# Attention and gated MLP on one core: pairs 4, 5 and 6 of batch 1 brought back to x^T by the transposing DMA in place of five transposes and a copy each

## The chip, the cores and the metric

The kernel runs on one core of a Trainium2 chip. The metric is device time in microseconds (us). Before the change: 323.52 us, the median of three runs (323.32 to 324.7). The program is one launch; its five engines (TensorE for matmuls, VectorE, ScalarE, GpSimd, and SyncE, which here only issues DMAs) each work through their own list of instructions and wait for one another by semaphores.

## The reference

Two layers follow each other. The first is causal attention with a sliding window of 128 and a linear bias, for 8 batches of 8 heads, 576 positions and 64 channels:

```
scores = q @ k^T / 8 - slope[h] * |i - j|      kept where 0 <= i - j < 128
attn   = exp(scores - max) / sum
x      = attn @ v        -> one row of 512 per token, 4608 tokens
```

The second is a gated MLP with 2048 hidden units:

```
h   = x @ w_in                   512 -> 2048
out = (h * clip(h + 3, 0, 6) / 6) @ w_out      2048 -> 512
```

## The kernel before

**Units.** Heads are taken two at a time. A *pair* g is batch g // 4 and heads 2(g % 4) and 2(g % 4) + 1; there are 32. Pairs 4 to 7 are batch 1, and `NP` is 4. For each pair the kernel makes the scores (TensorE), their exponentials (ScalarE), masks them (GpSimd), multiplies them with v (TensorE) and divides by the row sum (VectorE, L413 in `attend` for batches 0 and 1, L402 in `values` for the others). The divided tile is called `avs`: 128 tokens on the partitions, five blocks of tokens, two heads of 64 channels.

**Back to x^T.** The MLP wants x with channels on the partitions. `back(g)` (L421) turns `avs` into the rows of `xT` that belong to the pair, in one of two ways:
- by TensorE: five transposes of 128 x 128 into a PSUM tile (L432) and a copy from there into `xT` (L438; ScalarE, or VectorE for pair 7);
- by a transposing DMA from `avs` to `xT`, issued by SyncE (L425). It writes 640 columns, of which the last 64 are later overwritten by the next batch.

`by_xbar(g)` (L418) chooses: the DMA for pairs from 8 on, except 10 and 11; TensorE for all the others.

**Buffers.** `avs` comes from the pool `small`, which has two buffers in turn:

```
    small = ctx.enter_context(tc.tile_pool(name="small", bufs=2))
...
        avs = st[g, "avs"] = small.tile([128, NQ, 2, D], BF16, tag="avs", name="avs")
```

So `avs` of pair g takes the place of pair g - 2. The wide PSUM tiles of scores and values come from `ps_sc`, also two buffers; `wide_double` (L248, transposes of the next batch's q or k) uses the same pool.

**The MLP.** Tokens are taken 512 at a time (nt = 0 to 8). `up_mms` (L444) multiplies four blocks of 128 rows of `w_in` with four blocks of `xT`, one for each pair of a batch; L470 (ScalarE) and L471 (VectorE) make the gate; L501 is the second matrix; L510 and L511 copy and store the result. `up_begin(nt, ms, 3)` does the first three of the four blocks, and so reads the first three pairs of a batch. Tokens 512 to 1023 (nt = 1) need batch 1.

**Order.** The order of the work is written out by hand: inside `manual_schedule` every engine, SyncE among them, executes what the code gives it in the order of the code. The MLP's steps are laid between the attention's by `fill(n)`, which takes the next n steps of a fixed list and stops at a step whose batch isn't counted complete in `done[0]` (L528). `done` steers only this list, at the time the program is built.

**Around the change.** `second_batch` (L618) makes pairs 4 to 7. Ahead of the values it issues, in this order, on SyncE: v of batch 2 (L639, five loads), k of batch 3 (L642, four) and q of batch 3 (L643, five). The first of these waits for a one-column write by GpSimd (L638). Only then come the values and `back`:

```
        attend(NP)
        ...
        attend(NP + 1)
        fill(1)
        back(NP)
        attend(NP + 2)
        fill(1)
        back(NP + 1)
        double(2, 0, "k", 0, "av", A)
        attend(NP + 3)
        back(NP + 2)
        double(2, 0, "k", 1, "av", A)
        wide_double(2, 0, "q", A)
        up_begin(1, 0, 3)
        back(2 * NP - 1)
```

After that `segment` (L669) runs pairs 8 to 31. At its start for each g it sets `done[0] = g - 1` if pair g - 2 goes by the DMA.

Of the kernel before, what the change touches and what calls it, by code (L numbers as in the profile page):

```python
# [18 lines left out]
def kernel(  # L19
# [16 lines left out]
    NP = H // 2  # L36
# [11 lines left out]
    XB = 2 * NP  # L48
# [134 lines left out]
    def cast_tokens(b, nm):  # L183
        s = ld[b, nm]
        if nm == "v":
            for lo in (0, 2):
                nc.gpsimd.tensor_copy(  # L187
                    out=vbuf[b % 2][:, lo:lo + 2, :, 0:D].rearrange("p j h d -> p (j h) d"),
                    in_=s[:, lo:lo + 2, :, :].rearrange("p j h d -> p (j h) d"))
            nc.gpsimd.tensor_copy(out=vbuf[b % 2][:LAST, 4, :, 0:D], in_=s[:LAST, 4, :, :])  # L190
            return
        for j in range(NQ):
            m = min(128, S - j * 128)
            nc.gpsimd.tensor_copy(out=tbuf[:m, :, j, :],  # L194
                                  in_=s[:m, j, :, :].rearrange("p (i e) d -> p i (e d)", e=2))
# [40 lines left out]
    def double(b, dp, nm, part, tag, copy):  # L236
        src = st[b, dp, nm]
        t0, t1 = ((0, 5), (5, RT))[part]
        tp = BANKS[tag].tile([128, t1 - t0, 128], BF16, tag=tag, name="tp2",
                             padded_shape=[128, 8, 128])  # L240
        for t in range(t0, t1):
            nc.tensor.transpose(tp[:, t - t0, :], src[:, t, :], ident)
        dst = (qTb if nm == "q" else kTb)[b % 2][:, 2 * dp:2 * dp + 2, :, :]
        copy(out=dst.rearrange("p i j c -> p i (j c)")[:, :, 0:S].rearrange(  # L244
                 "p i (a t) -> p i a t", t=RT)[:, :, :, t0:t1],
             in_=tp.rearrange("p t (a i) -> p i a t", i=2))
# [83 lines left out]
    def scores(g):  # L330
        scores_diag(g)
        scores_off(g)
# [10 lines left out]
    def exp_diag(g, e):  # L343
        h = 2 * (g % NP) + e
        pd, sc = st[g, "pd"], st[g, "scd"]
        if diag_tabled(g):
            if e == 0:
                nc.scalar.activation(out=pd.rearrange("p e j c -> p e (j c)"), in_=sc,
                                     func=ACT.Exp, scale=scale)
            return  # L350
        nc.scalar.activation(out=pd[:, e, :, :].rearrange("p j c -> p (j c)"),  # L351
                             in_=sc[:, e, :], func=ACT.Exp,
                             bias=bias_d[:, h:h + 1], scale=scale)
        nc.gpsimd.affine_select(out=pd[:, e, :, :], in_=pd[:, e, :, :],  # L354
                                pattern=[[0, 4], [1, 128]], channel_multiplier=-1, base=0,
                                compare_op=ALU.is_ge, fill=0.0)

    def exp_off(g, e):
        h = 2 * (g % NP) + e
        po, sc, p4 = st[g, "po"], st[g, "sco"], p4buf[g % 2]  # L360
        nc.scalar.activation(out=po[:, e, :, :].rearrange("p j c -> p (j c)"),  # L361
                             in_=sc[:, e, :], func=ACT.Exp,
                             bias=bias_o[:, h:h + 1], scale=scale)
        nc.gpsimd.affine_select(out=po[:, e, :, :], in_=po[:, e, :, :],  # L364
                                pattern=[[0, 4], [-1, 128]], channel_multiplier=1, base=-1,
                                compare_op=ALU.is_ge, fill=0.0)
        nc.scalar.activation(out=p4[:, e, 0:64], in_=sc[:, e, 64:128], func=ACT.Exp,  # L367
                             bias=bias_d[:, h:h + 1], scale=scale)
        if e == 1:
            nc.gpsimd.affine_select(out=p4[:, :, 0:64], in_=p4[:, :, 0:64],  # L370
                                    pattern=[[0, 2], [1, 64]], channel_multiplier=-1, base=0,
                                    compare_op=ALU.is_ge, fill=0.0)
# [21 lines left out]
    def values(g, qts):  # L394
        av = ps_av.tile([128, 3, 2, W], FP32, tag="av", name="av", padded_shape=[128, 3, 2, 85])
        nq = len(qts)
        av_matmuls(g, qts, lambda qt, e: av[:, qt - qts[0], e, :])
        if qts[0] == 0:
            st[g, "avs"] = small.tile([128, NQ, 2, D], BF16, tag="avs", name="avs")
        rc = small.tile([128, 3, 2, 1], FP32, tag="rc", name="rc")  # L400
        nc.vector.reciprocal(rc[:, 0:nq, :, :], av[:, 0:nq, :, D:W])
        nc.vector.tensor_tensor(  # L402
            out=st[g, "avs"][:, qts[0]:qts[0] + nq, :, :], in0=av[:, 0:nq, :, 0:D],
            in1=rc[:, 0:nq, :, :].to_broadcast([128, nq, 2, D]), op=ALU.mult)
# [11 lines left out]
    done = [0]  # L416

    def by_xbar(g):  # L418
        return g >= XB and g != XB + 2 and g != XB + 3

    def back(g):  # L421
        b, hp = divmod(g, NP)
        avs = st[g, "avs"].rearrange("p j e d -> p j (e d)")
        if by_xbar(g):
            nc.sync.dma_start_transpose(  # L425
                out=xT[:, hp, ds(b % 4 * S, SP)].rearrange("p (j c) -> p j c", j=NQ),
                in_=avs.rearrange("p j c -> p (j c)"))
            return
        pool, tag = (ps_o, "o") if b < 2 else (ps_h, "h")
        tp = pool.tile([128, SP], BF16, tag=tag, name="tb", padded_shape=[128, 1024])  # L430
        for j in range(NQ):
            nc.tensor.transpose(tp[:, ts(j, 128)], avs[:, j, :], ident)  # L432
        if g == NP - 1:
            nc.scalar.copy(out=xT[:, hp, ds(b % 4 * S, 256)], in_=tp[:, 0:256])
            nc.vector.tensor_copy(out=xT[:, hp, ds(b % 4 * S + 256, S - 256)], in_=tp[:, 256:S])
            return
        eng = nc.vector.tensor_copy if g == 2 * NP - 1 else nc.scalar.copy
        eng(out=xT[:, hp, ds(b % 4 * S, S)], in_=tp[:, 0:S])  # L438
# [84 lines left out]
    def fill(n):  # L523
        for _ in range(n):
            if at[0] == len(units):
                return
            nt, fn, step = units[at[0]]
            if fn is moe_up and done[0] < NP * (min((nt * NT + NT - 1) // S, B - 1) + 1):  # L528
                return
            fn(nt if fn is moe_up else nt - 1, step)  # L530
            at[0] += 1
# [137 lines left out]
    def segment(lo, hi, fills):  # L669
        for g in range(lo, hi + 1):  # L670
            f = fills(g)
            if by_xbar(g - 2):
                done[0] = g - 1
            if lo < g < hi and g != 3 * NP + 1:
                scores(g)
            turn = {2 * NP: (2, 1, "k"), 2 * NP + 1: (2, 1, "q"),
                    2 * NP + 2: (3, 0, "k"), 2 * NP + 3: (3, 1, "k")}.get(g)
            if turn:
                double(*turn, 0, "av", A)
            fill(f[0])  # L680
            if turn:
                double(*turn, 1, *(("h", V) if turn[0] == 2 else ("av", A)))
            if g < hi:
                exp_diag(g, 0)
            fill(f[1])
            if g < hi:
                exp_diag(g, 1)
            if g == 3 * NP:
                cast_tokens(3, "v")
            if g > lo:  # L690
                values(g - 1, (0, 1, 2))
            fill(f[2])
            if g < hi:
                exp_off(g, 0)
            fill(f[3])
            if g < hi:
                exp_off(g, 1)
            if g > lo:
                values(g - 1, (3, 4))
            fill(f[4])  # L700
            if g > lo and by_xbar(g - 1):
                back(g - 1)
            fill(f[5])
            if g < hi:
                stage_next(g)
            fill(1)
            if g == 3 * NP:
                scores(g + 1)
            if g > lo and not by_xbar(g - 1):
                back(g - 1)  # L710
                done[0] = g
            fill(f[6] - 1)
# [51 lines left out]
```

## Time and profile before

| | |
|---|---|
| median of three runs | 323.52 us (323.32 to 324.7) |
| the profiled execution | 323.3 us, its span 321.6 us |
| granted TensorE clock over it | 0.998 |
| busy: TensorE / ScalarE / VectorE / GpSimd | 312.4 / 195.6 / 173.0 / 141.1 us |
| transposing DMAs to `xT` | 22, all on SyncE |
| transposes of `avs` on TensorE (L432) | 50, of 219 ns each as recorded |
| copies to `xT` after them (L438) | 8 on ScalarE, 639 ns; 1 on VectorE, 458 ns |

How to read the profile: times are microseconds from the span's start, unless marked ns. PE is TensorE, PEld its weight loads, DVE VectorE, ACT ScalarE, POOL GpSimd, SPq the instruction queue of SyncE. A row of the timeline gives the start, the length, the engine, the line of the kernel and the operation with its output and inputs, and, in brackets, how long the engine was idle before it and who released it. A row by stage gives the stage, its length, the busy time of TensorE, its weight loads, VectorE, ScalarE and GpSimd (with the number of instructions), the granted TensorE clock, the share of the DMA engines' time and GB/s. Recorded lengths of TensorE's matmuls overlap one another; the distance from one start to the next is what TensorE spends on one.

### The profile page before, as it was taken

The numbers are of one execution on the slowest core, as the hardware profiler recorded it, in microseconds if no ns is written. First come the engines' busy times: TensorE is split into PE (matmuls) and PEld (weight loads), VectorE is DVE, ScalarE is ACT, GpSimd is POOL, SyncE is SP. The second block draws the span as 40 slices with busy tenths as digits, with TensorE's granted clock in tenths as the row PEclk, the third lists the DMA queues.
The fourth block names the chain that finished last, engine by engine and source line by source line (L and its number), as shares of the span: only waits on it lengthen the run. The fifth ranks groups of instructions, "written<-read, shape, count | busy, mean of one in ns | idle before, by whom it ended". The sixth has DMA issues, their size and how long they took to land.

```text
span 321.6 us, 7050 instructions
## 1 busy us (share of the span) xinstructions
PE 312.4 (97%) x2738; PEld 167.6 (52%) x2738; DVE 173.0 (54%) x338; ACT 195.6 (61%) x334; POOL 141.1 (44%) x249
## 2 busy tenths in 40 slices
PE   7889999999999999999999999999999999999996
PEld 5565465455555554554667654554554444444443
DVE  6667674554456555555555555555655455455510
ACT  3758976877767766766676667666764344244401
POOL 8455493594493767366745665463331000000000
PEclk9999999999999999999999999999999999999999
DMA  7999999899999999999999989922112200000112
GB/s 276 202 333 208 247 270 196 210 258 194 212 248 166 244 201 203 193 229 199 192 199 202 237 173 212 214 72 86 23 53 66 75 34 35 33 33 33 67 53 77
DMA packets 131425, 51.90 MB, mean 161 GB/s; under 512 B 118976, under 2 KB 123328, under 8 KB 131392
## 3 DMA queue, kind: packets, MB, share of 16 engines
q1 hardware_dynamic: 126160, 45.36, 66.2%
q0 software_dynamic: 4224, 4.19, 8.2%
q10 hardware_dynamic: 1008, 1.90, 1.6%
q8 instruction: 21, 0.34, 0.5%
q14 instruction: 12, 0.10, 0.1%
HBM read 36.70 MB, written 9.44 MB: 143 GB/s over the span
## 4 chain that ended last, share of the span: by engine, by line
PE 82%; DMA 10%; SPq 2%; POOL 2%; DVE 1%; ACT 1%; issue 1%; POOLq 0%
PE ops L501 37%; PE hps L451 33%; DMA w_out_sb<-in_moe_w_out_dram 5%; DMA ldbuf<-in_v_dram 3%; PE scd L296 3%; DMA ldbuf<-in_k_dram 2%; PE av L391 2%; SPq L112 2%; PE av L383 2%; PE sco L328 1%; PE ops L482 1%; PE w L153 1%; POOL w_out_sb L171 1%; PE tp L219 0%; ACT kTb L244 0%
## 5 line engine op out<-in xcount | busy, mean ns | idle before, releaser
L471 DVE SCALAR_TENSOR_TENSOR gbuf<-r,hps 128x512 bf16<-128x512 f32 x144 | 98.7, 687 | 102.5 <-ACT r L470 100.2
L470 ACT ACTIVATE r<-hps,bias 128x512 f32<-128x512 f32 x144 | 98.9, 689 | 88.9 <-PE hps L451 88.7
L451 PE MATMUL hps<-xT,w_in_sb 128*128 128x512 bf16 (+1 forms) x640 | 144.8, 358 | 0.5 <-ACT xT L438 0.3
L501 PE MATMUL ops<-w_out_sb,gbuf 128*128 128x512 bf16 x560 | 137.8, 379 | 0.3 <-DMA w_out_sb<-in_moe_w_out_dram 0.3
L451 PEld LDWEIGHTS <-w_in_sb 128*128 128x128 bf16 x640 | 59.2, 98 | 54.8 <-issue 0.8
L501 PEld LDWEIGHTS <-gbuf 128*128 128x128 bf16 x560 | 51.8, 98 | 56.7 <-issue 0.6
L354 POOL TENSOR_SCALAR_AFFINE_SELECT pd<-pd 128x512 bf16<-128x512 bf16 x48 | 29.7, 634 | 34.5 <-ACT pd L351 34.5
L364 POOL TENSOR_SCALAR_AFFINE_SELECT po<-po 128x512 bf16<-128x512 bf16 x48 | 30.3, 636 | 32.5 <-ACT po L361 32.3
L351 ACT ACTIVATE pd<-scd,bias_d 128x512 bf16<-128x512 f32 x48 | 31.7, 685 | 4.7 <-PE scd L296 4.7
L510 DVE COPY osb<-ops 128x512 f32<-128x512 f32 x33 | 22.7, 687 | 20.4 <-PE ops L501 20.2
L361 ACT ACTIVATE po<-sco,bias_o 128x512 bf16<-128x512 f32 x48 | 33.0, 688 | 0.0
L194 POOL CAST tbuf<-ldbuf 128x512 bf16<-128x512 f32 (+1 forms) x45 | 25.6, 614 | 16.7 <-DMA qTb<-tbuf 9.0
L402 DVE TENSOR_TENSOR avs<-av,rc 128x384 bf16<-128x384 f32 (+1 forms) x48 | 23.6, 491 | 1.6
L391 PEld LDWEIGHTS <-pd 128*128 128x128 bf16 x192 | 14.3, 97 | 8.3 <-issue 0.5
L383 PE MATMUL av<-vbuf,po 128*128 128x65 bf16 x192 | 18.0, 193 | 0.0
L391 PE MATMUL av<-vbuf,pd 128*128 128x65 bf16 x192 | 17.3, 194 | 0.3 <-ACT kTb L244 0.3
L187 POOL CAST vbuf<-ldbuf 128x1024 bf16<-128x1024 f32 x14 | 14.3, 1044 | 4.3 <-DMA ldbuf<-in_v_dram 4.3
L383 PEld LDWEIGHTS <-po 128*128 128x128 bf16 x192 | 14.3, 98 | 2.9 <-DVE avs L402 0.5
L367 ACT ACTIVATE p4buf<-sco,bias_d 128x64 bf16<-128x64 f32 x48 | 15.5, 324 | 0.0
L227 POOL CAST pr<-ldbuf 128x576 bf16<-128x576 f32 x20 | 12.9, 670 | 5.0 <-DMA ldbuf<-in_k_dram 3.1
L296 PE MATMUL scd<-qTb,kTb 64*128 64x128 bf16 x256 | 12.7, 219 | 1.7 <-DVE kTb L220 0.9
L296 PEld LDWEIGHTS <-kTb 64*128 64x128 bf16 x256 | 7.2, 94 | 13.4 <-issue 9.7
(96 smaller groups left out, 217.4 us busy)
## 6 DMA issues: line engine op xcount, KB each, us to landing
out_dram<-osb SPq DMA_DIRECT2D x33, 256.0 KB, 2.4
ldbuf<-in_v_dram SPq DMA_DIRECT2D x32, 256.0 KB, 5.6
ldbuf<-in_q_dram SPq DMA_DIRECT2D x20, 256.0 KB, 4.9
ldbuf<-in_k_dram SPq DMA_DIRECT2D x16, 256.0 KB, 4.5
ldbuf<-in_q_dram SPq DMA_DIRECT2D x12, 288.0 KB, 7.3
ldbuf<-in_k_dram SPq DMA_DIRECT2D x12, 288.0 KB, 7.6
w_in_sb<-in_moe_w_in_dram POOLq DMA_DIRECT2D x4, 512.0 KB, 8.8
w_out_sb<-in_moe_w_out_dram POOLq DMA_DIRECT2D x4, 512.0 KB, 11.6
```

The source lines that it names most:

```text
L194: nc.gpsimd.tensor_copy(out=tbuf[:m, :, j, :], in_=s[:m, j, :, :].rearrange("p (i e) d -> p i (e d)", e=2))
L296: nc.tensor.matmul(scd[:, e, ts(j, 128)], lhsT=kT[r, j, :], rhs=qT[r, j, :], start=first, stop=first or j == 3)
L351: nc.scalar.activation(out=pd[:, e, :, :].rearrange("p j c -> p (j c)"), in_=sc[:, e, :], func=ACT.Exp, bias=bias_d[:, h:h + 1], scale=scale)
L354: nc.gpsimd.affine_select(out=pd[:, e, :, :], in_=pd[:, e, :, :], pattern=[[0, 4], [1, 128]], channel_multiplier=-1, base=0, compare_op=AL ...
L361: nc.scalar.activation(out=po[:, e, :, :].rearrange("p j c -> p (j c)"), in_=sc[:, e, :], func=ACT.Exp, bias=bias_o[:, h:h + 1], scale=scale)
L364: nc.gpsimd.affine_select(out=po[:, e, :, :], in_=po[:, e, :, :], pattern=[[0, 4], [-1, 128]], channel_multiplier=1, base=-1, compare_op=A ...
L383: nc.tensor.matmul(out_av, lhsT=po[:, e, qt % 4, :], rhs=vb[:, qt - 1, h, :], start=True, stop=False)
L391: nc.tensor.matmul(out_av, lhsT=d, rhs=vb[:, qt, h, :], start=(qt == 0), stop=True)
L451: nc.tensor.matmul(hps[:, lo:hi], lhsT=w_in_sb[:, ks, ts(ms, 128)], rhs=xT[:, ks, ds(src, hi - lo)], start=(ks == 0), stop=(ks == n_ks - 1))
L470: nc.scalar.activation(out=r6, in_=hps, func=ACT.Relu, bias=bias3[:, 0:1], scale=1.0 / 6.0)
L471: nc.vector.scalar_tensor_tensor(out=gts[nt][:, ms, :], in0=r6, scalar=1.0, in1=hps, op0=ALU.min, op1=ALU.mult)
L501: nc.tensor.matmul(ops[nt, sub], lhsT=gts[nt][:, ms, ts(sub, 128)], rhs=w_out_sb[:, ms, :], start=(ms == 0), stop=(ms == n_ms - 1))
```

## The change

`by_xbar` now holds for all pairs from 4 on except 7, 10 and 11. So `back(4)`, `back(5)` and `back(6)` each issue one transposing DMA on SyncE, where they had five transposes on TensorE and a copy on ScalarE. Pair 7 stays as it was. The second edit keeps `done[0]` from going back from 8 to 7 when `segment` starts with g = 8, for which pair 6 now answers True.

```
     def by_xbar(g):
-        return g >= XB and g != XB + 2 and g != XB + 3
+        return g >= NP and g not in (2 * NP - 1, XB + 2, XB + 3)
...
             if by_xbar(g - 2):
-                done[0] = g - 1
+                done[0] = max(done[0], g - 1)
```

`XB` is 8.

## The prediction

> **What bounds the kernel now.** I read the page first, then busy time by stage, then SyncE's own queue in the stretch that the change touches, with TensorE and VectorE beside it.
>
> ```profile
> span 321.6 us, 7050 instructions
> ...
> PE 312.4 (97%) x2738; PEld 167.6 (52%) x2738; DVE 173.0 (54%) x338; ACT 195.6 (61%) x334; POOL 141.1 (44%) x249
> ```
>
> TensorE is busy for 97% of the span. By stage:
>
> ```profile
> 50.00:60.00 10.00, 9.54 (x67) 4.55 (x65) 4.94 (x8) 7.40 (x14) 2.26 (x4) 1.00 1.06 188
> ...
> 70.00:80.00 10.00, 9.83 (x93) 5.18 (x88) 4.71 (x10) 7.27 (x13) 5.74 (x11) 1.00 1.17 201
> 80.00:100.00 20.00, 19.66 (x188) 10.26 (x187) 9.31 (x21) 14.51 (x29) 13.40 (x23) 1.00 1.11 228
> 100.00:250.00 150.00, 150.00 (x1308) 81.43 (x1306) 85.48 (x170) 99.35 (x183) 78.21 (x137) 1.00 0.86 166
> ```
>
> The second column is the stage's length, the third TensorE's busy time: from 50 to 250 us it lacks 0.46 + 0.17 + 0.34 = about 1 us (from 60 to 70 nothing). Whatever holds TensorE up at 50 us is therefore not made good later; it moves the end. Next, what SyncE issues around the second batch's values (start, length, operation):
>
> ```profile
> 38.52 1.33 SPq L98 DMA_DIRECT2D ldbuf<-in_q_dram  x2
> 47.95 11.95 SPq L112 DMA_DIRECT2D ldbuf<-in_v_dram  x5
> 59.96 3.29 SPq L98 DMA_DIRECT2D ldbuf<-in_k_dram  x4
> 63.30 5.75 SPq L112 DMA_DIRECT2D ldbuf<-in_q_dram  x5
> 69.16 0.57 SPq L511 DMA_DIRECT2D out_dram<-osb  x1
> 69.82 1.39 SPq L425 DMA_TRANSPOSE xT<-avs  x1
> ```
>
> SyncE goes strictly by the order of the code. The row that shows it is the store at 69.16: its tile was written by VectorE at 60.16 (0.68 us), so it lay ready for 8 us, behind the fourteen loads that the code issues before it. And what the three pairs have on VectorE and TensorE:
>
> ```profile
> 46.73 0.82 DVE L413 TENSOR_TENSOR avs<-wide,rcw 128x640 bf16<-128x640 f32 x1
> ...
> 60.16 0.68 DVE L510 COPY osb<-ops 128x512 f32<-128x512 f32 x1
> ```
>
> ```profile
> 44.44 0.45 PE L432 MATMUL tb<-ident,avs 128*128 128x128 bf16 x5
> ...
> 48.49 0.67 PE L254 MATMUL tp<-ident,pr 128*128 128x128 bf16 x9
> 48.99 0.81 PE L451 MATMUL hps<-xT,w_in_sb 128*128 128x512 bf16 x3
> ```
>
> The first hidden-layer matmuls that read pairs 4, 5 and 6 (`up_begin(1, 0, 3)`, three matmuls at L451) start at 48.99, right behind them.
>
> **What is removed.** Fifteen transposes on TensorE, five per pair. A group's share of TensorE runs from its start to the next group's: 44.44 to 44.73 for the one above, 0.29 us, so 0.87 us for three. Also three ScalarE copies of 0.64 us (L438), 1.9 us beside TensorE. All of it lies before 48.99. If something else sets when that matmul starts, this saving is worth nothing; I take 0, with a gain of 0.87 us as the other end.
>
> **What is added, and where.** Three transposing DMAs on SyncE, in code order behind the five v loads of batch 2, four k loads and five q loads of batch 3, which `second_batch` issues before `attend(NP)`. That queue is free of them at 63.30 + 5.75 = 69.05. Do the loads move? Their gate is GpSimd's one-column write at L638 at 47.8 (SyncE waited 7.5 us for it), and none waits for TensorE or VectorE work of this stretch, so a stalled TensorE neither delays nor hurries them. They go at the pace of the DMA rings, which are busy throughout (DMA share 1.06 from 50 to 60, and 1.07 from 60 to 70).
>
> A transposing DMA's own price stands in the trace:
>
> ```profile
> L425 SPq DMA_TRANSPOSE xT<-avs x22: 1200/1234/2051, 69.8 to 250.3; - x22
> ...
> DMA to landing us min/median/max: 2.4/2.5/4.3
> ```
>
> Issue 1.23 us, landing 2.4 to 4.3 us after the issue starts. The one at 69.82, behind the same loads, took 3.7.
>
> **What waits for it.** `avs` comes from a pool of two buffers. Pair 6's `avs` is pair 4's buffer, so VectorE's L413 of pair 6 (46.73 now) can't write until the DMA of pair 4 has landed. Behind it on VectorE are the gate products and pair 7's reciprocal and `avs`. TensorE is caught first by PSUM: `wide_double(2, 0, "q")` (L254, 48.49 now, about 47.7 without the transposes) takes the scores bank that pair 6's L413 has yet to read. Then L451 needs all three pairs landed. The chain:
> - DMA of pair 4 issued at 69.1, landed at 69.1 + 3.7 = 72.8. DMA of pair 5 is issued at 70.4 and lands beside it.
> - `avs` of pair 6: 0.82 us and two hand-overs, 73.7.
> - DMA of pair 6 from 73.75, the rings by now empty, so near the low end: 2.5 us, landed at 76.25.
> - L451 starts at 76.3 instead of 48.99: 27.3 us later. Pair 7's `avs` (75.4) and its transposes fit in.
>
> Ends for this term: all landings at 2.4 give 26.0 (69.1 + 2.4 + 0.95 + 2.4 = 74.9); both at 4.3 give 29.8.
>
> **What the pause costs besides.** TensorE stands still for some 27 us, apart from nine transposes at about 73.8. Rows of the start show what its first work costs:
>
> ```profile
> 1.43 2.31 PE L153 MATMUL w<-ident 128*128 128x128 bf16 x20 [1.43 <-POOL ident masks.py:199]
> ...
> 4.39 0.53 PE L307 MATMUL sco<-tab,ident 128*128 128x384 bf16 x1
> 4.71 0.31 PE L310 MATMUL sco<-tab,ident 128*128 128x128 bf16 x1
> ...
> 10.59 0.34 PE L307 MATMUL sco<-tab,ident 128*128 128x384 bf16 x1
> 10.76 0.22 PE L310 MATMUL sco<-tab,ident 128*128 128x128 bf16 x1
> ```
>
> The same 384-column matmul holds TensorE for 0.32 us at 4.39 and 0.17 us at 10.59. The slow pace lasts from 1.43 until somewhere in the second warm-up group (5.24 to 6.45): 3.8 to 5.0 us at about half pace, a loss of 1.9 to 2.5 us. I charge 2.2 us after the pause. The ends: 0 if the pace stays, since the page's granted clock reads 9 in every slice, the first too, and so says nothing of it; 3.5 if the slow stretch is longer. The Trainium skill, "TensorE: Matmul & The Clock Gate", Part 1, says the array falls to half clock after an idle window of some 3.4 us and comes back after a busy one. The start's pace agrees; that a pause brings it back, no row here shows. By one to two such windows, an estimate from that page, the sum would have 1.7 to 3.4 us in place of 2.2.
>
> **What is given back.** The w_out wait of 0.33 us at 59.05 goes, since those loads land at 59.0 regardless. What other idle there is after 50 us (0.7 us up to 100) mostly hangs on ScalarE work that moves along. SyncE would no longer be 9 us behind, but no wait of TensorE in this stretch was for it. I take 0.3, at most 1. The second edit (`max`) only keeps `done` at 8 when segment starts, where the new rule for pair 6 would set 7: no change in the order of work, cost 0.
>
> **Sum.** 27.3 + 2.2 - 0.3 = 29.2 us. The profiled execution took 323.3 us (span 321.6 and 1.7 around it), 0.2 below the median of 323.52. 323.3 + 29.2 = 352.5 us.
>
> **Rivals.**
> - Not slower: the transposing DMAs get to SyncE ahead of the loads, in its idle stretch from 39.85 (38.52 + 1.33) to 47.95. Then pair 4 is issued at 44.4 and lands by 46.9 at 2.5 us, pair 6's `avs` is at 47.7, its DMA lands at 50.2, and L451 is 1.2 us late, less 0.3 at w_out: 324.2 us, within what the measurement can tell (0.5%, 1.6 us). It decides if the issue precedes 47.95. For it speaks only that the queue is free there; against it, the store that lay ready for 8 us. Chance 3%, with 1% of it a gain, should the landing be wholly covered.
> - Slow landing: the DMAs find the rings as the loads did (v loads landed in up to 11.8 us; the transposing DMAs of batch tiles, larger, took a median of 6.4). At 7.5 us for pair 4 and 4.3 for pair 6 the chain ends at 69.1 + 7.5 + 0.95 + 4.3 = 81.9, 32.9 late: 358.1 us. Against it, 3.7 us in just this place. 7%.
> - No second trip: pair 6 does not wait for pair 4's landing. The third issue starts at 69.1 + 2 x 1.23 = 71.6 and lands, midway between 2.5 and 3.7 later, at 74.7: 25.7 late, 350.9 us with the other two terms as above. For it, nothing in the allocation of two buffers; 6%.
> - Short pause: the loads run ahead of their old times by several us with VectorE and TensorE still, say SyncE is free at 62 instead of 69: 345.5 us. Against it, the rings were full. 5%.
>
> **How the numbers follow.** The forecast has 79%. Its ends, 26.0 + 0 - 1 and 29.8 + 3.5, give 348.3 and 356.6; I set the range from 347 to 357, which also holds the rival without a second trip and leaves out about 15%. Slower by over 0.5%: 97%; within: 2%; faster: 1%.
>
> **What would show it.** Right: on VectorE an L413 that waits some 26 us for a DMA of `xT`; on SyncE three L425 issues directly behind the q loads, the first near 69.1; TensorE idle from about 48 to 74 before L254 and again for some 2 us before L451, then matmuls at half pace for 4 to 5 us; from there on the same rows as now, shifted by about 29 us. ScalarE without the three copies. Wrong: L425 rows near 44 to 48, landings well over 4 us, or stages after 100 us in which TensorE has less work or fewer gaps than now.

## The result and the profile after

The changed kernel takes 350.37 us (median of four runs, 348.22 to 352.19) against 323.82 us for the kernel before (four runs, 323.32 to 324.7). The ratio is 1.081, with a 95% interval of 1.074 to 1.089. The profiled execution took 351.13 us, 27.8 us more than that of the kernel before, and its span is 27.8 us longer as well.

The head of the page, with the rows for TensorE's busy time and granted clock in 40 slices:

```profile
span 349.4 us, 6988 instructions
...
PE 309.6 (89%) x2684; PEld 167.2 (48%) x2723; DVE 173.2 (50%) x338; ACT 194.5 (56%) x331; POOL 141.0 (40%) x249
...
PE   7888950049999999999999999999999999999996
...
PEclk9999995559999999999999999999999999999999
```

TensorE does the same work, apart from fifteen transposes, in 89% of the span instead of 97%. The loss lies in the gap in slices 6 to 9 (a slice is 8.7 us). The clock row shows a second thing: three slices at half clock, where the page of the kernel before has 9 throughout.

SyncE's queue in the stretch (start, length, operation):

```profile
48.81 11.43 SPq L112 DMA_DIRECT2D ldbuf<-in_v_dram  x5
60.29 2.57 SPq L98 DMA_DIRECT2D ldbuf<-in_k_dram  x4
62.91 6.42 SPq L112 DMA_DIRECT2D ldbuf<-in_q_dram  x5
69.43 5.89 SPq L425 DMA_TRANSPOSE xT<-avs  x3
```

The fourteen loads are within a microsecond of where they were, and the three transposing DMAs come right behind them, the first at 69.43. Its time from issue to landing:

```profile
xT<-avs SPq DMA_TRANSPOSE x1, 3.7
```

What that does to VectorE, and then to TensorE:

```profile
47.54 0.21 DVE L412 RECIPROCAL rcw<-wide 128x10 f32<-128x10 f32 x1
73.27 0.82 DVE L413 TENSOR_TENSOR avs<-wide,rcw 128x640 bf16<-128x640 f32 x1 [25.52 <-DMA xT<-avs]
```

```profile
48.89 0.38 PE L242 MATMUL tp<-ident,pr 128*128 128x128 bf16 x4 [0.29 <-ACT kTb L244]
74.15 1.12 PE L254 MATMUL tp<-ident,pr 128*128 128x128 bf16 x9 [24.88 <-DVE avs L413]
75.06 1.06 PE L451 MATMUL hps<-xT,w_in_sb 128*128 128x512 bf16 x2
76.54 0.58 PE L451 MATMUL hps<-xT,w_in_sb 128*128 128x512 bf16 x1 [0.42 <-DMA xT<-avs]
...
79.72 0.40 PE L296 MATMUL scd<-qTb,kTb 64*128 64x128 bf16 x8 [0.36 <-issue]
```

The brackets tell the chain. VectorE's division for pair 6 waits 25.5 us for the DMA that still has to read pair 4's `avs` out of the same buffer. TensorE waits 24.9 us for that division, because `wide_double` wants its PSUM bank. The last of the three first matmuls of batch 1 then waits another 0.42 us for the third DMA.

Busy time by stage (stage, length, TensorE, its weight loads, VectorE, ScalarE, GpSimd, then the granted clock, the DMA share and GB/s):

```profile
50.00:60.00 10.00, 0.00 (x0) 0.00 (x0) 0.00 (x0) 0.03 (x1) 1.21 (x2) 0.62 1.09 189
60.00:70.00 10.00, 0.00 (x0) 0.00 (x0) 0.00 (x0) 0.00 (x0) 0.00 (x0) 0.50 1.00 245
70.00:75.00 5.00, 0.85 (x9) 0.85 (x9) 1.70 (x4) 0.00 (x0) 0.00 (x0) 0.50 0.77 130
75.00:80.00 5.00, 4.22 (x27) 1.87 (x27) 1.14 (x2) 1.72 (x3) 0.00 (x0) 0.53 0.15 33
80.00:85.00 5.00, 4.87 (x44) 2.54 (x37) 2.65 (x4) 2.84 (x6) 0.64 (x1) 1.00 0.00 0
```

For twenty microseconds hardly any engine computes, and the DMA engines are full. From 75 to 80 TensorE works at half clock; then it is back.

### The profile page after: what moved, and what is told of

Its sections match the earlier page's. It is cut to its first block, busy times and chain, and to the rows that moved or that the text cites. A ratio compares the mean times of both kernels' runs of the same rounds, so it can differ in the third digit from the quotient of the medians.

```text
span 349.4 us, 6988 instructions
## 1 busy us (share of the span) xinstructions
PE 309.6 (89%) x2684; PEld 167.2 (48%) x2723; DVE 173.2 (50%) x338; ACT 194.5 (56%) x331; POOL 141.0 (40%) x249
## 4 chain that ended last, share of the span: by engine, by line
PE 74%; DMA 11%; SPq 7%; issue 2%; POOL 2%; ACT 1%; DVE 1%; ACTq 0%; POOLq 0%; DVEq 0%
PE ops L501 33%; PE hps L451 32%; SPq L112 7%; DMA ldbuf<-in_k_dram 3%; DMA w_in_sb<-in_moe_w_in_dram 3%; PE scd L296 2%; PE av L391 2%; DMA ldbuf<-in_q_dram 2%; DMA xT<-avs 2%; PE av L383 2%; PE sco L328 1%; DMA out_dram<-osb 1%; PE ops L482 1%; POOL pr L227 1%; SPq L98 1%
## 5 line engine op out<-in xcount | busy, mean ns | idle before, releaser
L451 PE MATMUL hps<-xT,w_in_sb 128*128 128x512 bf16 (+1 forms) x623 | 144.3, 360 | 3.0 <-DMA w_in_sb<-in_moe_w_in_dram 1.1
L501 PE MATMUL ops<-w_out_sb,gbuf 128*128 128x512 bf16 x538 | 133.8, 379 | 2.6 <-issue 2.1
L451 PEld LDWEIGHTS <-w_in_sb 128*128 128x128 bf16 x640 | 59.6, 98 | 56.5 <-issue 1.7
L501 PEld LDWEIGHTS <-gbuf 128*128 128x128 bf16 x560 | 51.8, 98 | 56.2
L354 POOL TENSOR_SCALAR_AFFINE_SELECT pd<-pd 128x512 bf16<-128x512 bf16 x48 | 29.8, 634 | 63.4 <-ACT pd L351 63.4
L254 PE MATMUL tp<-ident,pr 128*128 128x128 bf16 x45 | 3.8, 237 | 25.5 <-DVE avs L413 24.9
L413 DVE TENSOR_TENSOR avs<-wide,rcw 128x640 bf16<-128x640 f32 x8 | 6.6, 825 | 25.8 <-DMA xT<-avs 25.5
L254 PEld LDWEIGHTS <-pr 128*128 128x128 bf16 x45 | 3.2, 106 | 26.5 <-issue 25.0
```

What stands on the lines that cost most here:

```text
L451: nc.tensor.matmul(hps[:, lo:hi], lhsT=w_in_sb[:, ks, ts(ms, 128)], rhs=xT[:, ks, ds(src, hi - lo)], start=(ks == 0), stop=(ks == n_ks - 1))
L501: nc.tensor.matmul(ops[nt, sub], lhsT=gts[nt][:, ms, ts(sub, 128)], rhs=w_out_sb[:, ms, :], start=(ms == 0), stop=(ms == n_ms - 1))
```

## The experiments

**The theory** has three parts: the DMAs wait in SyncE's order behind fourteen loads; the two buffers of `avs` make the third wait for the first; and after the pause TensorE restarts slowly. The rivals are that the DMA engines are full there whatever the order, that the DMAs' own cost counts (so it would go with their number), and that the buffer is what costs. All runs are edits of the changed kernel. Ratios are against the kernel before as timed beside them, 323.2 to 323.8 us.

| run | us | ratio, 95% interval |
|---|---|---|
| the change | 350.37 | 1.074 to 1.089 |
| q loads behind the DMAs | 345.40 | 1.064 to 1.073 |
| pair 4 alone | 347.46 | 1.071 to 1.079 |
| four buffers | 349.23 | 1.075 to 1.085 |
| kept busy, 400 / 430 + 20 | 351.71 / 351.21 | 1.083 to 1.095 / 1.082 to 1.088 |
| issued by ScalarE | 339.60 | 1.046 to 1.051 |
| all loads behind the DMAs | 335.86 | 1.035 to 1.042 |
| the same, four buffers | 334.55 | 1.032 to 1.039 |
| the same, w_out issued later | 335.74 | 1.033 to 1.041 |
| the same, w_out after the DMAs | 335.88 | 1.037 to 1.041 |

### The place in SyncE's order: five of the fourteen loads

```
         for dp in range(2):
             load_double(3, dp, "k", nc.sync)
-        load_tokens(3, "q")
...
         back(NP + 2)
+        load_tokens(3, "q")
         double(2, 0, "k", 1, "av", A)
```

> Only the five q loads of batch 3 (6.4 us of SyncE's issue) go behind the three DMAs; v of batch 2 and k of batch 3 stay ahead. Theory (place in SyncE's order): the first transposing DMA is issued near 63 instead of 69.4, all that follows is 6 to 7 us earlier: 343 to 345 us. Rival (what counts is the DMAs' own cost, or the sum of the traffic): within 1.5 us of the changed kernel's 350.4.

Measured: 345.40 us, 5.0 less than the changed kernel, just above the expected 343 to 345. SyncE and TensorE:

```profile
61.32 7.44 SPq L425 DMA_TRANSPOSE xT<-avs  x3
```

```profile
67.58 1.12 PE L254 MATMUL tp<-ident,pr 128*128 128x128 bf16 x9 [19.50 <-DVE avs L413]
...
70.00 0.59 PE L451 MATMUL hps<-xT,w_in_sb 128*128 128x512 bf16 x1 [0.45 <-DMA xT<-avs]
...
72.38 0.40 PE L296 MATMUL scd<-qTb,kTb 64*128 64x128 bf16 x8
```

The first DMA is issued 8.1 us earlier than in the change (6.4 us of q loads, and in this execution the loads also began 1.9 us sooner), and TensorE's restart moves by 6.5 us with it. The first DMA took 5.3 us to land, against 3.7. From the last of the three matmuls at L451 to pair 8's scores at L296 it is 2.38 us here and 3.18 in the change; the 6.5 us and these 0.8 make up the 7.3 us between the two profiled executions (351.13 and 343.81). The rival, no change, is out.

### One DMA instead of three

```
-        return g >= NP and g not in (2 * NP - 1, XB + 2, XB + 3)
+        return (g >= XB and g not in (XB + 2, XB + 3)) or g == NP
```

> Pair 4 alone goes by the DMA, in place behind the fourteen loads; pairs 5 and 6 go back to five transposes and a copy each. Theory (place in SyncE's order): one DMA has to wait for the loads as long as three do, it lands near 73, and the division of pair 6 waits for it (two buffers); only the third DMA's trip of 2.5 us is gone: 347.5 to 349.5 us. Rival (the cost goes with the number of DMAs): a third of the loss of 27 us, near 332.

Measured: 347.46 us, at the lower end of the expected 347.5 to 349.5. One DMA costs 23.7 of the 26.6 us that three cost, so the loss does not go with their number. One part of the expectation was wrong. Pair 6's division did not wait:

```profile
51.23 0.82 DVE L413 TENSOR_TENSOR avs<-wide,rcw 128x640 bf16<-128x640 f32 x1
```

At 51.23 it can only write a buffer that the DMA, issued at 70.13, does not read. So the pool does not hand out its two buffers strictly in turn, and "pair g takes the place of pair g - 2" is no rule: with pair 5 brought back by TensorE, its buffer is free early, and pair 6 got that one. TensorE was caught at L451 directly:

```profile
73.80 1.44 PE L451 MATMUL hps<-xT,w_in_sb 128*128 128x512 bf16 x3 [20.41 <-DMA xT<-avs]
```

### Four buffers for avs

```
     small = ctx.enter_context(tc.tile_pool(name="small", bufs=2))
+    avsp = ctx.enter_context(tc.tile_pool(name="avsp", bufs=4))
...
-        avs = st[g, "avs"] = small.tile([128, NQ, 2, D], BF16, tag="avs", name="avs")
+        avs = st[g, "avs"] = avsp.tile([128, NQ, 2, D], BF16, tag="avs", name="avs")
```

and the same in `values`.

> avs has four buffers instead of two, all else as changed. Theory: the third DMA no longer waits for the first to land and for the division after it, so it is issued 2.5 us after the first, near 72, and lands near 74.7 instead of 76.5. TensorE is now caught at L451 alone, until then. Gain of 1 to 2 us on the changed kernel: 348.5 to 349.5 us. Rival (the double buffer is what holds TensorE up): a gain of 5 us or more, under 345.5 us.

Measured: 349.23 us, within the expected 348.5 to 349.5; but the interval overlaps that of the change, so the time alone does not settle it. The trace does (lines are one further down by the inserted line, so L452 is the change's L451):

```profile
71.56 1.12 PE L452 MATMUL hps<-xT,w_in_sb 128*128 128x512 bf16 x2 [21.87 <-DMA xT<-avs]
73.26 0.59 PE L452 MATMUL hps<-xT,w_in_sb 128*128 128x512 bf16 x1 [0.57 <-DMA xT<-avs]
```

SyncE came to the DMAs at 67.87 here, and the last matmul of the three starts 5.4 us later; in the change it was 7.1 us (69.43 to 76.54). The second trip is worth 1.7 us, not the pause. The rival, 5 us or more, is out.

### The slow restart

```
+        warm_up(400)
         wide_double(2, 0, "q", A)
         up_begin(1, 0, 3)
```

`warm_up(n)` issues n matmuls of the 128 x 128 identity with itself into a PSUM tile that nothing reads; this is work added.

> 400 matmuls of the identity with itself (128 x 128, results unused) are put in front of wide_double, so that TensorE works through the pause: at 0.058 us each they take 23 us of the 25. Theory (the pause costs its length and then a slow restart): the granted clock stays at 1.00, the matmuls behind the pause run at full pace, and the time falls by 1.5 to 2.5 us on the changed kernel: 348 to 349 us. Rival (no slow restart): 350.4 within 0.7.

Measured: 351.71 us, no gain, and as a test it failed. In the profiled execution, the slowest of the four (355.17), the DMAs came later (70.8), the added matmuls ended at 75.0, and between there and the restart the clock fell again:

```profile
77.02 0.66 PE L254 MATMUL tp<-ident,pr 128*128 128x128 bf16 x9 [2.04 <-DVE avs L413]
...
79.41 0.58 PE L451 MATMUL hps<-xT,w_in_sb 128*128 128x512 bf16 x1 [1.29 <-DMA xT<-avs]
```

The row from 80 to 85 us shows it:

```profile
80.00:85.00 5.00, 5.00 (x32) 2.31 (x31) 1.75 (x3) 1.26 (x2) 0.00 (x0) 0.50 0.00 0
```

So a second version filled the pause on both sides:

```
+        warm_up(430)
         wide_double(2, 0, "q", A)
+        warm_up(20)
         up_begin(1, 0, 3)
```

> The changed kernel with 430 idle matmuls of the identity in front of wide_double and 20 behind it, so that TensorE has no gap over 2 us in the pause. Theory (part of the cost is a slow restart): the granted clock stays at 1.00 behind the pause, and from the last of the three first matmuls at L451 to the first scores matmul of pair 8 it takes 1.7 us as in the kernel before, instead of 3.2. The time depends on when SyncE is done with the loads too, which varied by 2 us between executions; 348 to 350 us. Rival (no slow restart): 3.2 us there again.

Measured: 351.21 us, above the expected 348 to 350. The granted clock is 1.00 in every row behind the pause, and the stretch in question is short again:

```profile
78.45 0.38 PE L451 MATMUL hps<-xT,w_in_sb 128*128 128x512 bf16 x1 [0.19 <-DMA xT<-avs]
...
80.18 0.40 PE L296 MATMUL scd<-qTb,kTb 64*128 64x128 bf16 x8
```

From one to the other 1.73 us, against 3.18 us in the change (76.54 to 79.72) and also 3.18 us in the version with 400 matmuls (79.41 to 82.59), where the clock was down. In the kernel before, the three matmuls at L451 run from 48.99 to 49.64, some 0.217 us each, so the last starts at about 49.42, and pair 8's scores follow 1.74 us later:

```profile
49.64 0.44 PE L432 MATMUL tb<-ident,avs 128*128 128x128 bf16 x5
...
51.16 0.40 PE L296 MATMUL scd<-qTb,kTb 64*128 64x128 bf16 x8
```

The slow restart costs 1.45 us in the changed kernel. It is not the same in every execution: with the q loads behind the DMAs it was 0.65 (2.38 less 1.73). That the time as a whole did not fall is no contradiction: in this execution the last of the three matmuls started at 78.45 instead of 76.54, later by 1.91 us, which is more than the restart saved; the difference, 0.46, is about the 0.50 us by which this profiled execution (351.63) is longer than the change's. The DMAs were issued 0.7 us later (70.11), and the first took 5.0 us to land instead of 3.7. I did not test what set either.

### All loads behind the DMAs

```
-        load_tokens(2, "v")
         prepare_double(2, 1, (P, P))
-        for dp in range(2):
-            load_double(3, dp, "k", nc.sync)
-        load_tokens(3, "q")
...
         back(NP + 2)
+        load_tokens(2, "v")
+        for dp in range(2):
+            load_double(3, dp, "k", nc.sync)
+        load_tokens(3, "q")
```

> The fourteen loads of batches 2 and 3 are issued behind the three transposing DMAs instead of ahead of them. Theory (place in SyncE's order): the pause of 25 us goes. The first DMA is issued at about 44.6 us, lands 2.5 to 5 us later among the w_out traffic, the third lands at 52 to 55, so the first matmuls at L451 that read batch 1 are 3 to 6 us later than in the kernel before: 326 to 331 us. Rival (the rings are full in this stretch, wherever the DMAs stand in the queue): the DMAs are issued near 45 but land only when the w_out loads end, near 59, and the time stays above 338 us.

Measured: 335.86 us, above the theory's 326 to 331 and under the rival's 338. Half of the loss is gone, so the order was a cause; but the other half stayed. SyncE and TensorE, and the first DMA's time to landing:

```profile
44.71 12.40 SPq L425 DMA_TRANSPOSE xT<-avs  x3
57.21 4.86 SPq L112 DMA_DIRECT2D ldbuf<-in_v_dram  x5
```

```profile
55.94 1.12 PE L254 MATMUL tp<-ident,pr 128*128 128x128 bf16 x9 [7.73 <-DVE avs L413]
...
60.23 0.59 PE L451 MATMUL hps<-xT,w_in_sb 128*128 128x512 bf16 x1 [0.19 <-DMA xT<-avs]
```

```profile
xT<-avs SPq DMA_TRANSPOSE x1, 10.3
...
w_out_sb<-in_moe_w_out_dram POOLq DMA_DIRECT2D x4, 512.0 KB, 12.6
```

The DMA that took 2.4 to 4.3 us in the kernel before takes 10.3 us here, and the second 13.1. What is in flight beside them is GpSimd's 2 MB of w_out, issued from 40.8 on and landed by 59.3. My theory had lacked this price: ahead of the loads, the DMAs run into the w_out loads, which in the change had landed at 59.3, ten microseconds before the first DMA was issued. The next three runs test it.

### The same with four buffers

The two edits above together.

> The loads behind the three DMAs, as in the run that took 335.9 us, and four buffers for avs. Theory (the slow landing of some 10 us beside the w_out loads, paid once and a half, is what was left): all three are issued by 48 and land between 55 and 57, so the last of the three first matmuls at L451 starts near 56 instead of 60.2, and the time is 4 us less: 331 to 333 us. Rival (the landing ends with the w_out loads, whatever is queued when): 335 us or more.

Measured: 334.55 us, between the 331 to 333 that was expected and the rival's 335, and not told apart from 335.86 by the intervals; so the time decides nothing. In the trace the matmuls of pairs 5 and 6 start at 57.85 instead of the third at 60.23, so the second trip is some 2 us again; the landings themselves remain at 10 to 12 us.

### w_out issued behind GpSimd's casts

```
-        for i in range(4):
-            load_w_out(i)
...
         prepare_double(2, 1, (P, P))
+        for i in range(4):
+            load_w_out(i)
```

on top of the loads behind the DMAs, with two buffers.

> The loads behind the three DMAs, two buffers, and GpSimd issues the four w_out loads behind its casts of batch 2's q and k, some 6 us later. Theory (the DMAs land late because they share the DMA engines with the w_out loads): the first lands in 2.5 to 4 us, the third near 51 to 53 instead of 60.2; w_out itself is then late and TensorE waits for it at L501 instead, some 3 to 6 us: 327 to 333 us. Rival (a DMA between two SBUF tiles takes 10 us here for another reason): the first lands at 55 again, and the time is 336 us or more.

Measured: 335.74 us, neither what was expected (327 to 333) nor the rival's course. The trace holds both cases in one execution. The w_out loads are now issued later:

```profile
48.64 2.99 POOL L171 DMA_DIRECT2D w_out_sb<-in_moe_w_out_dram  x4
```

The first DMA, issued at 46.08, landed in 4.3 us. The second, issued about a microsecond before the loads, took 8.3. The third, issued about 51.3, when w_out was in flight:

```profile
xT<-avs SPq DMA_TRANSPOSE x1, 9.9
```

I had expected w_out to come late enough for all three; it caught the last two.

### w_out only after the DMAs

```
+        nc.gpsimd.memset(xT[:, 2, ds(2 * S, 1)], 0.0)
+        for i in range(4):
+            load_w_out(i)
```

behind `back(NP + 2)` and ahead of the moved loads, in place of the four at their old place. The one column belongs to batch 2 and is written again later; until then it is part of the 64 columns that the third DMA writes too far, so GpSimd waits for that DMA.

> The fourteen loads behind the three DMAs, and GpSimd issues the w_out loads only when the third DMA has landed. Theory (the slow landing is shared DMA engines): with nothing else in flight but the last q loads of batch 2, the first lands in 2.5 to 4.5 us, the third near 52 to 55; w_out comes some 9 to 12 us later than before and TensorE waits for it at L501: 329 to 336 us, with waits for w_out in place of those for xT. Rival: landings of 8 us or more again, and both waits: 338 us or more.

Measured: 335.88 us, within the expected 329 to 336, with waits for w_out as expected. With w_out out of the way the DMAs landed in 4.2, 3.5 and 2.4 us; the first:

```profile
xT<-avs SPq DMA_TRANSPOSE x1, 4.2
```

TensorE:

```profile
52.26 0.58 PE L451 MATMUL hps<-xT,w_in_sb 128*128 128x512 bf16 x1 [1.34 <-DMA xT<-avs]
...
60.63 1.89 PE L501 MATMUL ops<-w_out_sb,gbuf 128*128 128x512 bf16 x4 [4.78 <-DMA w_out_sb<-in_moe_w_out_dram]
...
71.36 1.02 PE L501 MATMUL ops<-w_out_sb,gbuf 128*128 128x512 bf16 x4 [1.68 <-DMA w_out_sb<-in_moe_w_out_dram]
```

The third of the first matmuls is only 2.8 us later than in the kernel before (52.26 against about 49.42), but w_out is late in turn, and the sum is the same. So the slow landings come from the w_out loads in flight beside them, and either the one waits or the other. Why these loads cost a DMA more than SyncE's own, beside which it took up to 5.3 us, no run shows.

### Another issuing engine

```
-            nc.sync.dma_start_transpose(
+            (nc.scalar if b == 1 else nc.sync).dma_start_transpose(
```

> The changed kernel with batch 1's three transposing DMAs issued by ScalarE instead of SyncE; the loads stay where they are. Theory (two parts: SyncE's order, then the engines shared with the w_out loads): the wait for SyncE is gone, the DMAs are issued from 45 on, but land in some 10 us as with the loads behind them: 334 to 338 us, with ScalarE held up by the issues besides. Rival (the ring of SyncE is what is full, another ring is free): landing in 2.5 to 4.5 us, 325 to 330 us.

Measured: 339.60 us, somewhat above the expected 334 to 338; the rival's 325 to 330 is out. ScalarE's queue and the landing of the first DMA on it:

```profile
45.64 1.40 ACTq L425 DMA_TRANSPOSE xT<-avs  x1
...
57.55 1.22 ACTq L425 DMA_TRANSPOSE xT<-avs  x1
```

```profile
xT<-avs ACTq DMA_TRANSPOSE x1, 11.0
```

The first is issued at 45.64, 24 us earlier than in the change, with the loads untouched, and lands in 11.0 us; the third, issued at 57.55, in 7.0. A free queue gets round SyncE's order, but not round the traffic. The Trainium skill, "DMA: Bandwidth & Descriptors", section "Issuing engines are not separate DMA queues", says that DMAs from ScalarE, SyncE and GpSimd end up on the same DMA engines and interleave; this run agrees, with 11.0 us from ScalarE beside 10.3 from SyncE.

No order that I tried beats the kernel before; the best, 334.55 us, is 3.5% slower.

## Why the prediction was right

The forecast was 352.5 us, with a range of 347 to 357; measured were 350.37, and 351.13 for the profiled execution that its terms stand against. The ends of its first term come to 25.9 and 29.7 by its own figures, not 26.0 and 29.8; nothing hangs on that.

- **SyncE's order** was the step that carried it, and it held: free of the loads at 69.05 by the forecast, 69.33 in the trace; the first two issues right behind them, the third when VectorE had written. The run with the five q loads moved and the one with all fourteen behind show it as a cause. That the time agrees to 0.3 us is in part luck: in the other executions profiled with the loads in their old place SyncE came to the DMAs between 67.9 and 70.8.
- **The landing** of the first, taken as 3.7 us: 3.7. The third, taken as 2.5: issued when VectorE had written (74.1), landed 2.4 us later at 76.5.
- **VectorE held by the buffer, TensorE by the bank**: 25.5 us at L413 and 24.9 us at L254, as described. That pair 6 must take pair 4's buffer held in this kernel, but the run with one DMA shows that it is not so of itself. The four-buffer run sizes the second trip at 1.7 us; the rival without a second trip had 1.6 (25.7 instead of 27.3).
- **The pause**: 27.3 us forecast for L451. The last of the three matmuls moved from 49.4 to 76.54, which is 27.1.
- **The slow restart** was the term that I mis-sized, 2.2 us. From L451 to pair 8's scores the shift grew from 27.1 to 28.56 (51.16 to 79.72), which is 1.4, and the run kept busy has 1.45. The mechanism was right: the half clock lasted from the restart at 74.15 to about 79.7, and the forecast had 4 to 5 us of it. Part of the slow work, the nine transposes of L254 and two of the three matmuls, lay under the wait for the third DMA, and so cost nothing. I had charged the whole slow stretch to the path.
- **What is given back**, 0.3 us: the shift went from 28.56 to 27.8 at the end of the span, 0.76 us. The w_out wait went, as said, and was worth some 0.5: the four L451 matmuls before it and the L501 behind it start 1.35 us apart before (57.70, 59.05) and 0.86 after (86.26, 87.12). From pair 9's scores (61.73, 89.81) to TensorE's last group (314.82, 342.88) the shift stays at 28.1, so the last 0.26 lies behind TensorE's work. The lower busy time of TensorE after 100 us, which the forecast had named as a sign of being wrong, is therefore no loss: the trace lacks records (from 100 to 250 us it has 1333 matmuls for 1352 weight loads).
- **The saved transposes**, 0.87 us, gave nothing, since the end of the pause was set by SyncE.

27.1 + 1.44 - 0.76 is 27.8, the difference of the two profiled executions. The forecast's 29.2 was over by 0.2 in the pause, 0.8 in the restart and 0.5 in what is given back. The rival on the other side, DMAs that get ahead of the loads and land in 2.5 us for 324.2 us, fell on both counts. The order kept them behind the loads. And where an experiment did put them ahead, the landing was 10.3 us, a price that this rival had too low: its 2.5 came from DMAs issued from 69.8 us on, with w_out long landed.

The forecast said that the granted clock, 9 in every slice before, tells nothing of the slow pace. Behind the pause it does: 0.50 to 0.53. The Trainium skill, "TensorE: Matmul & The Clock Gate", Part 1, puts the fall to half clock at one idle window of some 3.4 us. The trace is near that: the clock fell between 52 and 53 us, about 3.1 us after the last transpose of 48.89 had ended. The other runs do not show it as a fixed delay: it was 2.6 us with four buffers and 4.4 with one DMA, and on ScalarE's queue the clock fell at 51.5, 0.3 us after four transposes that followed a gap of 1.5.

## What to carry to other kernels

Work taken from a busy engine onto a DMA is paid in latency, and its start is set by what stands ahead of it in the issuing queue: look up when that queue is free before counting what is saved. A landing time holds only for the traffic beside which it was read; the same DMA cost 2.4 us at the least, and 10 to 14 in the middle of the w_out loads. Here three DMAs that could save 0.87 us of TensorE lay between divisions and a first reader that stood only 1.4 to 4.6 us apart, and none of the placements tried could hide them.

## What the runs showed of the hardware

- A transposing DMA between two SBUF tiles, 2.4 to 4.3 us in the kernel before, took 9.9 to 14.0 us when it was issued with all four 512 KB loads of w_out in flight or just being issued, from SyncE's queue (9.9 to 13.1) and from ScalarE's (11.0 and 14.0) alike. Towards their end it took less: 4.3 us when issued 3.4 us before the last of them landed, 7.0 when issued 3.7 us before.
- After the pause the half clock cost 1.45 us on the path, and 0.65 in the run with the q loads behind. TensorE need not be idle without a break for the clock to fall: in the run with 400 matmuls, after 24 us of dense work, it fell at about 78.3, 3.3 us after the last of them, though 1.1 us of matmuls lay between (0.64 from 78 to 79, 0.50 from 80 to 85).
- Executions of the changed kernel lie 4.0 us apart (348.22 to 352.19), those of the kernel before 1.4. In the executions profiled with the loads in their old place, SyncE came to the DMAs at 67.9, 69.4, 70.1, 70.1 and 70.8, and the five v loads had begun at 47.4, 48.8, 50.4, 49.5 and 49.6. With the pause, differences in when the DMAs land reach TensorE. That this is why the times spread more, and the whole of it, was not tested.
